# Taps of a state-space convolution: each channel's samples side by side in both factors

## The chip, the cores and the metric

The kernel runs on one core of one Trainium2 chip, as one launch. The metric is the device time of that launch in microseconds, the median of three runs. A core has TensorE (PE in the profile), VectorE (DVE), ScalarE (ACT), GpSimd (POOL) and SyncE (SP). Each works through its own instructions in order, and semaphores tie them together.

## The reference, cut to what matters

Two branches work on the same 2048 x 512 input and are mixed row by row with a sigmoid gate.

```python
g = sigmoid((x * gate_w).sum(-1, keepdims=True))
# branch a: a long convolution, one filter of 2048 taps for each of D = 512 channels
logdA, dB = dt * (A_re + 1j * A_im), dt * (B_re + 1j * B_im)   # (512, 128)
P = exp(logdA[:, :, None] * l)                                 # (512, 128, 2048)
K = einsum("dn,dnl,dn->dl", C, P, dB).real                     # the taps
a = irfft(rfft(u, 2L) * rfft(K, 2L))[:L] + u * Dskip
# branch b: a dense layer of 1792 hidden units
b = gelu(x @ w1 + b1) @ w2 + b2
out = g * a + (1 - g) * b
```

The change concerns the taps `K`. For each channel they are a sum over 128 states of a complex power, and the position l is split in two: l = 64 p + s, with 32 values of p and 64 of s. A power at l is then the product of a power at 64 p (times the coefficients) and a power at s, so that the sum over the states is a matrix product for each channel: 32 rows (p) by 64 columns (s), contracted over 128 states in the partitions, once for the real parts and once for the imaginary parts.

## The kernel before, in words

The program has a front part and a convolution part. In the front part (to about 400 us in the profile) two jobs run beside each other. The dense branch keeps TensorE busy: hidden products (lines 985 to 987, three for each because a factor is split into a high and a low part), a gelu and a cast to the high part on ScalarE (lines 1002 and 1005), the low part on VectorE (line 1012), and output products (lines 1028 to 1031). The other job makes the taps, in 16 groups of 32 channels (`CW`). The convolution part (from about 400 us) transforms taps and signal, multiplies them and transforms back.

One group of taps goes through these functions:

- `phases` (VectorE, line 695): multiples of a state's angle, as integers, in the tile `ph`, 33 samples by 32 channels.
- `waves` (ScalarE, lines 711 to 713): an Abs, a Sin and a second Sin turn the 33 x 32 phases into cosines and sines in the tile `tt`. The last of the three works in place in `tt`.
- `magnitudes` (VectorE, lines 750 and 752; GpSimd, line 740): the magnitudes of the powers, doubled from 2 to 64 samples, in `e`, which is the half `y[:, 1]` of the tile `y`.
- `rotate` (VectorE, lines 763, 770 and 774): magnitude times cosine into `y[:, 0]`, magnitude times sine into `y[:, 1]`.
- `begin` (ScalarE, line 721) and `powers` (VectorE, lines 594 to 597 in `cmul`): the other factor in `xc`, 32 samples by 32 channels for the real and for the imaginary part, doubled from 4 samples to 32. `xc` lies in the rows of `den`; there are two, used in turn. `xt_` and `xv_`, in `loft`, hold the partial products.
- `contract` (TensorE, line 788): for each of the 32 channels two matrix products, with 32 columns of `xc` as the weights and 64 columns of `y` as the moving data. Four channels at a time stand on four tiles of 32 columns of the array. In the profile each product of 32-bit floats is two instructions, so that a group (a block of `contract`) has 32 x 2 x 2 = 128 and there are 2048 in all. They are issued as two tasks of 64, which follow each other in one stretch of 3.84 us.

In the tiles `y`, `xc` and `tt` the sample is the outer index and the channel the inner one: for one channel, two consecutive samples lie 32 words (128 bytes) apart.

The order of the work in the front part is that of a planner: every task has a due time from a table of numbers (`DUES`) and a cost, and a run through the costs settles the order on every engine. A task's instructions are issued in that order, and each waits for its semaphores. The due times, the costs and the tasks' dependencies are the same in the changed kernel.

Of the kernel before, what the change touches and what calls it, by code (L numbers as in the profile page):

```python
# [9 lines left out]
F32 = mybir.dt.float32  # L10
# [7 lines left out]
P = 128  # L18
# [331 lines left out]
def gated_mix(  # L350
# [52 lines left out]
    def front(pool, psum, keep, attic, loft, den, pr):  # L403
# [29 lines left out]
        pus = tiles(N_PU, [P, D], "pu", space=psum)  # L433

        sk = pool.tile([P, 64, 2, 4, 8], F32, name="sk")
        y = pool.tile([P, 2, 64, CW], F32, name="y")
        xc = [den[:, k : k + 4].rearrange("p k d -> p (k d)").rearrange("p (a b c) -> p a b c", a=2, c=CW) for k in (0, 4)]
        xt_, xv_ = (loft[:, k * 1024 : k * 1024 + 1024].rearrange("p (a b c) -> p a b c", a=2, c=CW) for k in range(2))
        tt = loft[:, 2048:4160].rearrange("p (a b c) -> p a b c", a=2, c=CW)
        ph = pool.tile([P, 33, CW], I32, name="phase")  # L440
        zz = pool.tile([P, 2, 5, UW], F32, name="zz")
        x4 = pool.tile([P, 2, 4, UW], F32, name="x4")
# [142 lines left out]
            )  # L585
            vec(UW, lambda: v.tensor_copy(dtb, pus[1][:, 0:UW]), -190, [("pu", 1)], ["dtb"])

        def cmul(due, dst, a, br, bi, n, t, v, ka, kb, kd, kt, kv):

            w = a.shape[-1]  # L590
            br = br.unsqueeze(1).unsqueeze(1).to_broadcast([P, 2, n, w])
            bi = bi.unsqueeze(1).unsqueeze(1).to_broadcast([P, 2, n, w])
            vv, m = nc.vector, n * w
            vec(2 * m, lambda: vv.tensor_mul(t, a, br), due, [ka, *kb], [kt])  # L594
            vec(2 * m, lambda: vv.tensor_mul(v, a, bi), due, [ka, *kb], [kv])  # L595
            vec(m, lambda: vv.tensor_sub(dst[:, 0], t[:, 0], v[:, 1]), due, [kt, kv], [kd])
            vec(m, lambda: vv.tensor_add(dst[:, 1], t[:, 1], v[:, 0]), due, [kt, kv], [kd])
# [110 lines left out]

        def waves(t):
            def sines():  # L710
                nc.scalar.activation(tt[:, 0], ph, AF.Abs)
                nc.scalar.activation(tt[:, 1], ph, AF.Sin, scale=TWO_PI / TURN)
                nc.scalar.activation(tt[:, 0], tt[:, 0], AF.Sin, bias=half_pi, scale=-TWO_PI / TURN)  # L713

            act(3.14, sines, t + D_KA, ["ph"], ["tt"], "sin")

        def begin(c, k, t):

            cs = slice(c * CW, (c + 1) * CW)
            act(  # L720
                0.31, lambda: nc.scalar.copy(xc[k][:, :, 0:4], x4[:, :, :, cs]), t + D_KA,
                ["x4"], [("xc", k)],
            )
# [13 lines left out]
        def magnitudes(u, c, t):  # L737

            cs = slice(c * CW, (c + 1) * CW)
            pl.add("POOL", 0.1, lambda: nc.gpsimd.memset(e[:, 63], 1.0), t, [], ["y1"])  # L740

            def both(lo, step, n):

                a = e[:, lo : lo + n].copy()
                return bass.AP(a.tensor, a.offset, [a.ap[0], [step * CW, 2], *a.ap[1:]])

            def double(k):
                n = 1 << k
                an = ea[u % 2][:, k, cs].unsqueeze(1).unsqueeze(1).to_broadcast([P, 2, n, CW])
                nc.vector.tensor_mul(both(n, 64 - 3 * n, n), both(0, 64 - n, n), an)  # L750

            vec(CW, lambda: nc.vector.tensor_copy(e[:, 0], ea[u % 2][:, 5, cs]), t, [("ea", u % 2)], ["y1"])
            for k in range(5):
                vec(2 * CW << k, lambda k=k: double(k), t, [("ea", u % 2)], ["y1"])

        def rotate(t):

            v = nc.vector
            cc = tt[:, 0, 0:32]
            cc = bass.AP(cc.tensor, cc.offset, [cc.ap[0], [CW, 2], *cc.ap[1:]])  # L760

            def real():
                v.tensor_mul(  # L763
                    y[:, 0].rearrange("p (a b) c -> p a b c", a=2),
                    e.rearrange("p (a b) c -> p a b c", a=2),
                    cc,
                )

            def imag0():
                v.scalar_tensor_tensor(e[:, 0:32], e[:, 0:32], -1.0, tt[:, 1, 0:32], ALU.mult, ALU.mult)  # L770

            vec(64 * CW, real, t, ["tt", "y1"], ["y0"])
            vec(32 * CW, imag0, t, ["tt"], ["y1"])
            vec(32 * CW, lambda: v.tensor_mul(e[:, 32:64], e[:, 32:64], tt[:, 1, 1:33]), t, ["tt"], ["y1"])

        pair = []

        def contract(u, c, k, t):
# [4 lines left out]
            def products(g0):  # L783
                for gg in range(g0, g0 + 4):
                    for r in range(2):
                        for j in range(4):
                            ch = j * 8 + gg
                            nc.tensor.matmul(  # L788
                                pks[q][32 * j : 32 * j + 32, :, gg],
                                x[:, r, :, ch],  # L790
                                y[:, r, :, ch],
                                start=(r == 0),
                                stop=(r == 1),
                                skip_group_check=True,
# [679 lines left out]
```

## Time and profile before

| | |
|---|---|
| median of 3 runs | 508.46 us (508.36 to 508.69) |
| span of the profiled execution | 505.5 us |
| time around that span, against the median | 2.96 us |
| TensorE busy | 495.2 us, 98% of the span |
| VectorE busy | 429.2 us, 85% |
| ScalarE busy | 365.0 us, 72% |
| GpSimd busy | 38.3 us, 8% |
| granted clock of TensorE, mean | 0.996 |

No separate total is kept for the profiled execution, so that its own time is taken as its span and 2.96 us around it, which makes it the median. The profile names an instruction by its line, its engine, and the tile that it writes and those that it reads (out<-in). `den` in such a name can be `xc`, and `loft` can be `tt`, `xt_` or `xv_`, as these share memory. Busy shares over the whole span are means over a front part and a convolution part that have different limits; the stage from 24 to 380 us is the one in which the taps are made. The lengths of TensorE's instructions overlap, and their ends are modelled, so that distances between starts say more than lengths.

### The profile page before, as it was taken

The numbers are of one execution on the slowest core, as the hardware profiler recorded it, in microseconds if no ns is written. First come the engines' busy times: TensorE is split into PE (matmuls) and PEld (weight loads), VectorE is DVE, ScalarE is ACT, GpSimd is POOL, SyncE is SP. The second block draws the span as 40 slices with busy tenths as digits, with TensorE's granted clock in tenths as the row PEclk, the third lists the DMA queues.
The fourth block names the chain that finished last, engine by engine and source line by source line (L and its number), as shares of the span: only waits on it lengthen the run. The fifth ranks groups of instructions, "written<-read, shape, count | busy, mean of one in ns | idle before, by whom it ended". The sixth has DMA issues, their size and how long they took to land.

```text
span 505.5 us, 12181 instructions
## 1 busy us (share of the span) xinstructions
PE 495.2 (98%) x4802; PEld 379.0 (75%) x4802; DVE 429.2 (85%) x817; ACT 365.0 (72%) x632; POOL 38.3 (8%) x78
## 2 busy tenths in 40 slices
PE   8999999999999999999999999999999999999994
PEld 7898888898989889888988888998989522222551
DVE  4977999999999999999999999999940197877455
ACT  6999997899997789997767998636834465565310
POOL 2000000000000000001010020110100100231000
PEclk9999999999999999999999999999999999999998
DMA  8978686531858622855987244950477999989897
GB/s 286 350 280 278 188 243 213 161 126 43 280 138 246 200 73 72 254 168 116 232 217 241 75 64 128 186 100 3 154 219 169 259 389 389 338 305 391 294 344 299
DMA packets 81569, 107.56 MB, mean 213 GB/s; under 512 B 39284, under 2 KB 43784, under 8 KB 80968
## 3 DMA queue, kind: packets, MB, share of 16 engines
q1 hardware_dynamic: 74792, 82.80, 51.8%
q0 software_dynamic: 6016, 20.70, 15.4%
q10 hardware_dynamic: 704, 3.28, 1.8%
q8 instruction: 38, 0.62, 0.5%
q14 instruction: 19, 0.16, 0.1%
HBM read 61.14 MB, written 45.62 MB: 211 GB/s over the span
## 4 chain that ended last, share of the span: by engine, by line
PE 93%; DMA 2%; SPq 1%; DVE 1%; issue 1%; ACT 0%; POOL 0%; DVEq 0%; POOLq 0%
PE pk L788 12%; PE ph L985 10%; PE acc L1028 10%; PE ph L987 10%; PE ph L986 10%; PE acc L1029 9%; PE acc L1031 9%; PE p2k L1218 5%; PE p2u L1218 5%; PE pa L1257 3%; PE ph L489 3%; PE pb L1373 2%; DMA tk<-tk_d 1%; SPq L830 1%; DMA tk_d<-sk 1%; PE acc L1101 1%
## 5 line engine op out<-in xcount | busy, mean ns | idle before, releaser
L985 PE MATMUL ph<-xh,wh 128*128 128x256 f32 x448 | 127.5, 285 | 0.0
L987 PE MATMUL ph<-xh,wl 128*128 128x256 f32 x448 | 126.8, 283 | 0.0
L986 PE MATMUL ph<-xlo,wh 128*128 128x256 f32 x448 | 126.7, 283 | 0.0
L985 PEld LDWEIGHTS ph<-xh,wh 128*128 128x128 f32 x448 | 85.2, 190 | 6.9 <-issue 4.0
L986 PEld LDWEIGHTS ph<-xlo,wh 128*128 128x128 f32 x448 | 85.1, 190 | 2.1
L987 PEld LDWEIGHTS ph<-xh,wl 128*128 128x128 f32 x448 | 85.2, 190 | 0.0
L1028 PE MATMUL acc<-wh,hh 128*128 128x512 f32 x208 | 84.3, 405 | 0.0
L1029 PE MATMUL acc<-wl,hh 128*128 128x512 f32 x208 | 81.7, 393 | 0.0
L1031 PE MATMUL acc<-wh,hl 128*128 128x512 f32 x208 | 81.4, 391 | 0.0
L1002 ACT ACTIVATE ph<-ph,b1t 128x256 f32<-128x256 f32 x112 | 50.5, 451 | 25.0 <-PE ph L987 23.2
L788 PE MATMUL pk<-y,den 128*32 128x64 f32 x2048 | 61.4, 290 | 0.0
L788 PEld LDWEIGHTS pk<-y,den 128*32 128x32 f32 x2048 | 57.2, 136 | 2.6 <-issue 0.7
L1012 DVE TENSOR_TENSOR hl<-ph,hh 128x512 fp32r<-128x512 f32 (+1 forms) x62 | 38.2, 618 | 18.3 <-ACT hh L1005 10.8
L1028 PEld LDWEIGHTS acc<-wh,hh 128*128 128x128 f32 x208 | 39.1, 188 | 19.4 <-issue 8.8
L750 DVE TENSOR_TENSOR y<-y,ea 128x64 f32<-128x64 f32 (+4 forms) x80 | 45.3, 566 | 0.8 <-POOL y L740 0.3
L1031 PEld LDWEIGHTS acc<-wh,hl 128*128 128x128 f32 x208 | 39.1, 188 | 8.8
L1029 PEld LDWEIGHTS acc<-wl,hh 128*128 128x128 f32 x208 | 39.1, 188 | 6.1
L1226 ACT COPY k<-p2k 128x512 f32<-128x512 f32 x32 | 18.6, 586 | 27.2 <-issue 11.3
L594 DVE TENSOR_TENSOR loft<-den,zz 128x256 f32<-128x256 f32 (+2 forms) x48 | 37.2, 774 | 0.2
L595 DVE TENSOR_TENSOR loft<-den,zz 128x256 f32<-128x256 f32 (+2 forms) x48 | 37.2, 775 | 0.1
L763 DVE TENSOR_TENSOR y<-y,loft 128x2048 f32<-128x2048 f32 x16 | 36.6, 2286 | 0.4 <-ACT loft L713 0.2
L1005 ACT CAST hh<-ph 128x512 fp32r<-128x512 f32 (+1 forms) x62 | 33.0, 533 | 4.3 <-PE acc L1029 2.4
(197 smaller groups left out, 873.3 us busy)
## 6 DMA issues: line engine op xcount, KB each, us to landing
tk_d<-sk SPq DMA_DIRECT2D x32, 256.0 KB, 5.3
t_d<-sa SPq DMA_DIRECT2D x32, 256.0 KB, 5.1
tu_d<-attic SPq DMA_DIRECT2D x40, 128.0 KB, 3.5
attic<-in_xt_dram SPq DMA_DIRECT2D x16, 256.0 KB, 4.3
attic<-in_xs_dram SPq DMA_DIRECT2D x16, 256.0 KB, 5.0
xl_d<-xlo SPq DMA_DIRECT2D x8, 512.0 KB, 5.9
xh_d<-xh SPq DMA_DIRECT2D x8, 512.0 KB, 3.9
out_dram<-io SPq DMA_DIRECT2D x16, 256.0 KB, 3.1
```

Source lines behind the costliest of these rows:

```text
L594: vec(2 * m, lambda: vv.tensor_mul(t, a, br), due, [ka, *kb], [kt])
L750: nc.vector.tensor_mul(both(n, 64 - 3 * n, n), both(0, 64 - n, n), an)
L788: nc.tensor.matmul(pks[q][32 * j : 32 * j + 32, :, gg], x[:, r, :, ch], y[:, r, :, ch], start=(r == 0), stop=(r == 1), skip_group_check=True,)
L985: nc.tensor.matmul(p, h, xh[xk][:, d], start=(d == 0), stop=False)
L986: nc.tensor.matmul(p, h, xlo[xk][:, d], start=False, stop=False)
L987: nc.tensor.matmul(p, lo, xh[xk][:, d], start=False, stop=(d == 3))
L1002: nc.scalar.activation(phs[q][:, n], phs[q][:, n], AF.Gelu_apprx_tanh, bias=b1t[:, f : f + 1])
L1012: nc.vector.tensor_sub(lo, phs[q][:, 0:nf], hi.bitcast(F32))
L1028: nc.tensor.matmul(a, h, wh[1][w], start=start, stop=False, skip_group_check=seeded)
L1029: nc.tensor.matmul(a, h, wl[1][w], start=False, stop=False, skip_group_check=seeded)
L1031: nc.tensor.matmul(a, l, wh[1][w], start=False, stop=stop, skip_group_check=seeded)
L1218: nc.tensor.matmul(out[64 * i : 64 * i + 64], w, x, start=True, stop=True)
```

## The change

Channel and sample change places in `y`, `xc`, `xt_`, `xv_` and `tt`: the channel is now the outer index, and the samples of one channel lie side by side. The phases stay as they were, sample by channel; the first two instructions of `waves` read them as before and write their results turned, so that consecutive elements of their output lie 33 words (132 bytes) apart. `begin` turns the four starting samples in the same manner, 32 words apart. In `cmul` and `magnitudes` the factor that is the same for all samples of a channel is now repeated in the innermost index and no longer over whole rows of channels. The doubling steps of `magnitudes` and `powers` write runs of 1, 2, 4, 8 and 16 samples per channel, where they wrote runs of 32 channels. `contract` reads 32 weights and 64 moving columns side by side.

No instruction is added or taken away, and on every engine all instructions stand in the same order as before.

```diff
-        y = pool.tile([P, 2, 64, CW], F32, name="y")
-        xc = [den[:, k : k + 4]....rearrange("p (a b c) -> p a b c", a=2, c=CW) for k in (0, 4)]
-        xt_, xv_ = (loft[...].rearrange("p (a b c) -> p a b c", a=2, c=CW) for k in range(2))
-        tt = loft[:, 2048:4160].rearrange("p (a b c) -> p a b c", a=2, c=CW)
+        y = pool.tile([P, 2, CW, 64], F32, name="y")
+        xc = [den[:, k : k + 4]....rearrange("p (a c b) -> p a c b", a=2, c=CW) for k in (0, 4)]
+        xt_, xv_ = (loft[...].rearrange("p (a c b) -> p a c b", a=2, c=CW) for k in range(2))
+        tt = loft[:, 2048:4160].rearrange("p (a c b) -> p a c b", a=2, c=CW)
...
-        def cmul(due, dst, a, br, bi, n, t, v, ka, kb, kd, kt, kv):
-            w = a.shape[-1]
-            br = br.unsqueeze(1).unsqueeze(1).to_broadcast([P, 2, n, w])
-            bi = bi.unsqueeze(1).unsqueeze(1).to_broadcast([P, 2, n, w])
+        def cmul(due, dst, a, br, bi, n, t, v, ka, kb, kd, kt, kv, inner=False):
+            w = CW if inner else a.shape[-1]
+            shape, at = ([P, 2, w, n], 3) if inner else ([P, 2, n, w], 1)
+            br = br.unsqueeze(1).unsqueeze(at).to_broadcast(shape)
+            bi = bi.unsqueeze(1).unsqueeze(at).to_broadcast(shape)
...
         def waves(t):
             def sines():
-                nc.scalar.activation(tt[:, 0], ph, AF.Abs)
-                nc.scalar.activation(tt[:, 1], ph, AF.Sin, scale=TWO_PI / TURN)
+                to = [tt[:, i].rearrange("p c b -> p b c") for i in range(2)]
+                nc.scalar.activation(to[0], ph, AF.Abs)
+                nc.scalar.activation(to[1], ph, AF.Sin, scale=TWO_PI / TURN)
                 nc.scalar.activation(tt[:, 0], tt[:, 0], AF.Sin, bias=half_pi, scale=-TWO_PI / TURN)
...
-                0.31, lambda: nc.scalar.copy(xc[k][:, :, 0:4], x4[:, :, :, cs]), t + D_KA,
+                0.31, lambda: nc.scalar.copy(xc[k][:, :, :, 0:4].rearrange("p a c b -> p a b c"), x4[:, :, :, cs]), t + D_KA,
...
                 cmul(
-                    t, x[:, :, n : 2 * n], x[:, :, 0:n], zz[:, 0, i, cs], zz[:, 1, i, cs], n,
-                    xt_[:, :, 0:n], xv_[:, :, 0:n], ("xc", k), ["zz"], ("xc", k), "xt", "xv",
+                    t, x[:, :, :, n : 2 * n], x[:, :, :, 0:n], zz[:, 0, i, cs], zz[:, 1, i, cs], n,
+                    xt_[:, :, :, 0:n], xv_[:, :, :, 0:n], ("xc", k), ["zz"], ("xc", k), "xt", "xv", True,
                 )
...
-                return bass.AP(a.tensor, a.offset, [a.ap[0], [step * CW, 2], *a.ap[1:]])
+                return bass.AP(a.tensor, a.offset, [a.ap[0], [step, 2], *a.ap[1:]])
...
-                an = ea[u % 2][:, k, cs].unsqueeze(1).unsqueeze(1).to_broadcast([P, 2, n, CW])
+                an = ea[u % 2][:, k, cs].unsqueeze(1).unsqueeze(3).to_broadcast([P, 2, CW, n])
...
-            vec(CW, lambda: nc.vector.tensor_copy(e[:, 0], ea[u % 2][:, 5, cs]), t, [("ea", u % 2)], ["y1"])
+            vec(CW, lambda: nc.vector.tensor_copy(e[:, :, 0], ea[u % 2][:, 5, cs]), t, [("ea", u % 2)], ["y1"])
...
-                                x[:, r, :, ch],
-                                y[:, r, :, ch],
+                                x[:, r, ch],
+                                y[:, r, ch],
```

`rotate` has the same three instructions on the turned tiles: the cosine of sample b is read for the samples b and 32 + b at once, the second with an offset of one sample.

More of the change, by code (lines that the diff above doesn't have):

```diff
@@ L435, in front @@
         sk = pool.tile([P, 64, 2, 4, 8], F32, name="sk")
-        y = pool.tile([P, 2, 64, CW], F32, name="y")
-        xc = [den[:, k : k + 4].rearrange("p k d -> p (k d)").rearrange("p (a b c) -> p a b c", a=2, c=CW) for k in (0, 4)]
-        xt_, xv_ = (loft[:, k * 1024 : k * 1024 + 1024].rearrange("p (a b c) -> p a b c", a=2, c=CW) for k in range(2))
-        tt = loft[:, 2048:4160].rearrange("p (a b c) -> p a b c", a=2, c=CW)
+        y = pool.tile([P, 2, CW, 64], F32, name="y")
+        xc = [den[:, k : k + 4].rearrange("p k d -> p (k d)").rearrange("p (a c b) -> p a c b", a=2, c=CW) for k in (0, 4)]
+        xt_, xv_ = (loft[:, k * 1024 : k * 1024 + 1024].rearrange("p (a c b) -> p a c b", a=2, c=CW) for k in range(2))
+        tt = loft[:, 2048:4160].rearrange("p (a c b) -> p a c b", a=2, c=CW)
         ph = pool.tile([P, 33, CW], I32, name="phase")
```

16 lines of the change are left out of this document (8 added, 8 removed).

## The prediction

> **What bounds the kernel now.** I read the page's totals first, then the busy time by stage, then groups of instructions by shape, then single places on the time line, then the waits.
>
> ```profile
> span 505.5 us, 12181 instructions
> PE 495.2 (98%) x4802; PEld 379.0 (75%) x4802; DVE 429.2 (85%) x817; ACT 365.0 (72%) x632; POOL 38.3 (8%) x78
> ...
> 24.00:60.00 36.00, 35.97 (x244) 32.15 (x242) 30.67 (x76) 35.35 (x62) 0.53 (x1) 1.00 0.80 265
> 60.00:100.00 40.00, 40.00 (x488) 32.74 (x472) 39.61 (x84) 34.15 (x55) 0.25 (x2) 1.00 0.67 205
> 100.00:140.00 40.00, 40.00 (x500) 35.53 (x492) 39.17 (x81) 38.98 (x71) 0.30 (x2) 1.00 0.47 149
> 140.00:180.00 40.00, 40.00 (x471) 34.64 (x471) 39.51 (x74) 30.34 (x50) 1.85 (x5) 1.00 0.66 181
> 180.00:220.00 40.00, 40.00 (x481) 34.87 (x480) 39.16 (x70) 39.29 (x75) 1.30 (x4) 1.00 0.50 153
> 220.00:260.00 40.00, 40.00 (x379) 33.43 (x378) 39.15 (x80) 29.94 (x48) 5.86 (x9) 1.00 0.74 178
> 260.00:300.00 40.00, 40.00 (x588) 36.11 (x587) 38.04 (x69) 34.95 (x62) 2.59 (x7) 1.00 0.47 134
> 300.00:340.00 40.00, 40.00 (x360) 35.24 (x360) 39.31 (x80) 27.23 (x43) 6.50 (x10) 1.00 0.65 135
> 340.00:380.00 40.00, 40.00 (x591) 34.92 (x590) 31.38 (x51) 24.02 (x36) 3.12 (x6) 1.00 0.45 130
> ```
>
> The columns are the window, then TensorE, its weight loads, VectorE, ScalarE and GpSimd busy, the granted clock and the DMA. The share over the span (VectorE 85%, ScalarE 72%) hides what matters: from 24 to 380 us, the stage that the change touches, TensorE is never idle, and from 60 to 340 us VectorE is busy for 273.95 of 280 us (39.61 + 39.17 + 39.51 + 39.16 + 39.15 + 38.04 + 39.31). So two engines are full at once, and the third, ScalarE, is full in two windows (38.98 and 39.29 of 40). Its 61.75 us of idle time from 24 to 380 lie in the others. The chain of waits runs over TensorE for 93%, but time saved on TensorE alone is worth no more than VectorE's idle time, 6.05 us in those seven windows.
>
> **The change part by part.** No instruction is added, removed or put elsewhere; only access patterns differ. So every term is a count of elements by a price per element. The rows by shape:
>
> ```profile
> L788 PE MATMUL pk<-y,den 128*32 128x64 f32 x2048 | 61.4, 290 | 0.0
> L763 DVE TENSOR_TENSOR y<-y,loft 128x2048 f32<-128x2048 f32 x16 | 36.6, 2286 | 0.4 <-ACT loft L713 0.2
> L594 DVE TENSOR_TENSOR loft<-den,zz 128x1024 f32<-128x1024 f32 x16 | 19.5, 1221 | 0.1
> L774 DVE TENSOR_TENSOR y<-y,loft 128x1024 f32<-128x1024 f32 x16 | 19.5, 1219 | 0.0
> L713 ACT ACTIVATE loft<-loft,half_pi 128x1056 f32<-128x1056 f32 x16 | 18.7, 1169 | 0.0
> L712 ACT ACTIVATE loft<-phase 128x1056 f32<-128x1056 int32 x16 | 17.5, 1094 | 0.2
> L711 ACT ACTIVATE loft<-phase 128x1056 f32<-128x1056 int32 x16 | 17.5, 1093 | 0.0
> L1269 ACT COPY sa<-pa 128x512 f32<-128x512 f32 x32 | 17.2, 589 | 9.5 <-PE pa L1257 5.4 <-issue 4.1
> L815 ACT COPY sk<-ph 128x512 f32<-128x512 f32 x8 | 4.7, 593 | 0.0
> L659 ACT ACTIVATE loft<-loft 128x768 f32<-128x768 f32 x4 | 3.4, 854 | 0.0
> L721 ACT COPY den<-x 128x256 f32<-128x256 f32 x16 | 6.2, 407 | 11.5 <-PE pk L788 8.1 <-DVE x L597 3.4
> ```
>
> And six pieces of TensorE's time line (start, length, line):
>
> ```profile
> 71.61 3.84 PE L788 MATMUL pk<-y,den 128*32 128x64 f32 x128
> 99.08 0.65 PE L489 MATMUL ph<-s,c1t 32*64 32x512 f32 x2
> 99.10 0.65 PE L489 MATMUL pk<-s,c1t 32*64 32x512 f32 x2
> 99.11 0.66 PE L489 MATMUL pu<-s,c1t 32*64 32x512 f32 x4
> 420.85 1.03 PE L1218 MATMUL p2k<-t,cc 128*64 128x512 f32 x4
> 421.71 1.03 PE L1218 MATMUL p2k<-t,f 128*64 128x512 f32 x4
> ```
>
> *TensorE.* A block of L788 is 128 instructions on four column tiles, 32 each, 64 columns each: 2048 columns per tile. Less the last one's 0.29 us the block takes 3.55 us, so 1.73 ns per column, and each column is read 128 bytes from the one before. L1218 reads columns side by side: four instructions on two tiles start 0.86 us apart from the next four, so 1024 columns per tile in 0.86 us, 0.84 ns each. At that price a block is 2048 x 0.84 = 1.72 us, and 1.83 us shorter: 29.3 us of TensorE's time over 16 blocks. The other end is nothing, if the pace is that of issue: 3.55 / 128 = 28 ns per instruction. I take the gain, since L489 issues eight instructions between 99.08 and 99.11 us, far faster than 28 ns each.
>
> [...]
>
> *What a hop costs.* From the same rows: an element that lies far from the one before costs 1.73 ns on a read, where neighbours cost 0.84 on TensorE, 1.04 on VectorE ((2286 - 1219) / 1024) and 0.83 on ScalarE ((1094 - 854) / 288). No row shows a write that hops at every element; L815 writes runs of eight at 593 ns against 589 for L1269 in one run, so runs cost nothing.
>
> *ScalarE.* L711 and L712 now write 1056 elements each with 132 bytes from one to the next, L721 256 elements with 128 bytes. L713 stays in one run. If a hopping write is bound like the hopping read, the extra is 1.73 - 0.83 = 0.90 ns: 2 x 1056 x 0.90 + 256 x 0.90 = 2.13 us in each of 16 groups, 34.1 us in all. The other end is nothing. I take 0.90: 1.73 ns is twice what TensorE needs for neighbours, so I read it as a limit of the memory that is read and not of the engine, and such a limit should hold for a write too.
>
> [...]
>
> *What of it reaches the end.* ScalarE is off the chain only as long as it keeps ahead. Its groups of sines by window, and what stands behind one:
>
> ```profile
> 24.00:60.00 36.00, 1.09 (x1) 1.00 0.80 265
> 100.00:140.00 40.00, 2.19 (x2) 1.00 0.47 149
> 180.00:220.00 40.00, 1.11 (x1) 1.00 0.50 153
> 260.00:300.00 40.00, 2.34 (x3) 1.00 0.47 134
> ...
> 152.10 1.16 ACT L713 ACTIVATE loft<-loft,half_pi 128x1056 f32<-128x1056 f32 x1
> 154.58 0.93 ACT L1002 ACTIVATE ph<-ph,b1t 128x256 f32<-128x256 f32 x2
> 155.54 0.59 ACT L1005 CAST hh<-ph 128x512 fp32r<-128x512 f32 x1
> ...
> DVE hl L1012 <- ACT hh L1005: 10.8, 9, 3.5
> ACT ph L1002 <- PE ph L987: 23.2, 12, 6.0
> ACT io L1053 <- PE acc L1031: 10.8, 10, 4.0
> ```
>
> Lower end: each window first uses up its own idle time. 24-60: 2.13 against 0.65 idle; 100-140: 4.26 against 1.02; 180-220: 2.13 against 0.71; 260-300: 6.39 against 5.05. The overflows are 1.48 + 3.24 + 1.42 + 1.34 = 7.5 us; the other windows hold it. Upper end: all 34.1. Behind each group of sines stand the gelu (L1002) and the cast (L1005) of the dense part; VectorE's L1012 and TensorE's L1028 and L1031 wait for them. VectorE works in order and has no idle time to make up a lost microsecond, and it already waits for that cast (10.8 us in nine waits). Much of ScalarE's idle time is its wait for TensorE (23.2 and 10.8 us), which moves along when TensorE is late. So I take two thirds, 23 us.
>
> *VectorE.* L752 (32 elements) now writes single elements and the smallest L750 (64) reads and writes them: (32 + 128) x (1.73 - 1.04) ns = 0.11 us, 1.8 us over 16 groups, from 0 to twice that. The other L750 and L594/L595 keep runs of 2 to 16 in their long operands, which I cost at nothing by L815, but their factor is now read n times over before the next one. No row shows a word read again and again in the innermost place; a factor repeated over whole rows costs nothing (L594 1221 against L774 1219). Bounds: 0, and 0.69 ns for each of 128 + 256 + 512 + 1024 + 2 x (256 + 512 + 1024) = 5504 elements, 3.8 us per group, 61 us. I take 0, as the nearest row is L594. The rotations (L763, L770, L774) read rows of 33 words in runs of 32: nothing.
>
> *Sum.* 505.5 + 23 (ScalarE) + 1.8 (VectorE) = 530.3; off it goes what the shorter blocks give, at most VectorE's 6.05 us less its own 1.8, of which I count 3: 527.3 us of span. The runs' median is 508.46, 2.96 above this execution's span, so 530 us. Blocks shorter by 29 us of TensorE are hidden behind VectorE; what is late next is the hidden layer's cast.
>
> **The rivals.**
>
> *ScalarE's writes hop for free* (the other side). Then only TensorE's blocks change and VectorE decides. The point from which it decides is the price of a hopping write: under about 0.1 ns extra, 4 us over 16 groups, all hidden. The time is 508.5 - 6.05 + 1.8 = 504, and 502 if VectorE's small steps cost nothing. For it: no row shows a write of that kind to be slow. Against it: the reads' 1.73 ns. [...]
>
> *The repeated factor costs VectorE.* 61 us of VectorE work less 6 of idle: 508.5 + 55 = 563, and ScalarE then has time to hide its own. For it: single elements cost on the other reads; against it: the same word lies in the same place.
>
> *The change does not do what it says*: blocks of L788 stay at 3.8 us because issue sets them. With free writes 508.5 + 1.8 = 510, with ScalarE's price 533.
>
> **How the numbers follow.** ScalarE's price as taken: 0.52, of itself from 514 (7.5 us passed on, less 3) to 545 (34.1 and 1.8), likeliest 530. Free writes and shorter blocks: 0.24, 502 to 507. Free writes and unchanged blocks: 0.06, about 508 to 510. The repeated factor: 0.14, 555 to 575. The rest, 0.04, is a hop price well above 1.73 ns. The range of 503 to 545 leaves out the repeated factor and the rest. 0.2%, about 1 us, is what a measurement of this kernel can tell from no change. Faster: 0.24 and a little of the unchanged blocks, 0.26. Same: 0.05. Slower: 0.69.
>
> **What would show it.** L711 and L712 near 2.0 us (1094 + 1056 x 0.90), L721 near 0.64, L713 still 1.17. L788's blocks near 2.0 us with 128 instructions. L750 with 64 elements near 0.3 us, its larger shapes and L594/L595 unchanged. TensorE with idle time before L1028 and L1031, put down to ScalarE or VectorE, and VectorE's wait for L1005 above 10.8 us. Wrong if L711 stays near 1.1 us (then 504), or if L594 with 1024 elements goes towards 1.9 us (then 563).

## The result, and the profile after

| | before | after |
|---|---|---|
| median of 4 runs | 508.57 us (508.36 to 509.12) | 527.04 us (524.96 to 528.95) |
| span of the profiled execution | 505.5 us | 523.2 us |

The kernel is slower: the ratio is 1.0369 (95% interval 1.0334 to 1.0404), 18.5 us. The profiled execution of after took 524.96 us by its own clock, 1.76 us around its span. In the changed kernel the lines from 594 to 710 are one further on than before (L594 is now L595), and the lines from 711 on two (L711 is L713, L788 is L790, L1005 is L1007). In the experiments lines are up to three further on than before in the same manner.

The totals of the page and the chain that ended last, then TensorE, weight loads, VectorE, ScalarE and GpSimd busy with granted clock from 60 to 340 us:

```profile
span 523.2 us, 12185 instructions
PE 479.7 (92%) x4802; PEld 352.2 (67%) x4802; DVE 430.7 (82%) x817; ACT 400.5 (77%) x632; POOL 38.7 (7%) x78
ACT 46%; PE 29%; DVE 11%; issue 6%; DMA 4%; SPq 1%; POOL 0%; ACTq 0%; DVEq 0%; POOLq 0%
60.00:340.00 280.00, 251.99 (x3031) 207.21 (x3032) 259.36 (x498) 257.03 (x390) 15.10 (x32) 0.99 0.55 156
```

The chain ran over TensorE for 93% before; now ScalarE has 46% of it and TensorE 29%. The counts of these engines' instructions are as before; the four more in the total (12185 against 12181) are none of theirs. ScalarE works 35.5 us more in all (400.5 against 365.0), VectorE 1.5 us more, TensorE 15.5 us less. From 60 to 340 us TensorE was busy for all 280 us and VectorE for 273.95; now they are busy for 252 and 259. Both have idle time, and ScalarE isn't full over the whole stretch either (257.03 of 280). So no single engine is the limit by its total: all three wait for one another, and ScalarE's lateness is handed round. The groups by shape show where its time comes from (busy time, mean ns of one, then the idle time ahead):

```profile
L713 ACT ACTIVATE loft<-phase 128x1056 f32<-128x1056 int32 x16 | 36.0, 2249 | 1.3 <-DVE phase L696 1.3
L714 ACT ACTIVATE loft<-phase 128x1056 f32<-128x1056 int32 x16 | 35.8, 2236 | 0.2
L715 ACT ACTIVATE loft<-loft,half_pi 128x1056 f32<-128x1056 f32 x16 | 18.2, 1140 | 0.0
L723 ACT COPY den<-x 128x256 f32<-128x256 f32 x16 | 10.2, 675 | 3.8 <-DVE x L598 3.4 <-PE pk L790 0.4
L790 PE MATMUL pk<-y,den 128*32 128x64 f32 x2048 | 32.8, 220 | 4.1 <-DVE y L776 2.2 <-ACT attic L507 1.7
L595 DVE TENSOR_TENSOR loft<-den,zz 128x1024 f32<-128x1024 f32 x16 | 19.5, 1219 | 0.1
L752 DVE TENSOR_TENSOR y<-y,ea 128x1024 f32<-128x1024 f32 x16 | 19.5, 1218 | 0.1
L752 DVE TENSOR_TENSOR y<-y,ea 128x64 f32<-128x64 f32 x16 | 4.3, 269 | 0.3
L754 DVE COPY y<-ea 128x32 f32<-128x32 f32 x16 | 3.1, 194 | 0.0
```

The two writes that hop 132 bytes at each element went from 1093 and 1094 to 2249 and 2236 ns; L715, which writes the same tile in one run, stayed (1169 before, 1140 now). The extra is (2249 - 1093) / 1056 = 1.09 ns an element, and in `begin` (675 - 407) / 256 = 1.05. Lengths say a little too much here, since ScalarE's instructions overlap (the two rows of before below by 0.11 us, those of after by 0.26). A group whose sines follow each other directly, of before and of after on the time line:

```profile
127.70 1.10 ACT L711 ACTIVATE loft<-phase 128x1056 f32<-128x1056 int32 x1
128.69 1.09 ACT L712 ACTIVATE loft<-phase 128x1056 f32<-128x1056 int32 x1
```

```profile
134.17 2.27 ACT L713 ACTIVATE loft<-phase 128x1056 f32<-128x1056 int32 x1
136.18 2.28 ACT L714 ACTIVATE loft<-phase 128x1056 f32<-128x1056 int32 x1
```

From start to start it is 0.99 us and 2.01 us: (2.01 - 0.99) / 1056 = 0.97 ns an element is what the next instruction feels. This is so for the second of the two in every group, but for the first in this group alone: in the other 15 an ACT_TABLE_LOAD of 1.28 us stands between the two and starts only when the first has ended, so that the first costs its whole length there. ScalarE's busy time, in which an overlap counts once, grew by 35.5 us where the lengths of the three groups grew by 40.8. VectorE's products with the factor repeated in the innermost place (L595, and L752 with 1024 elements) kept their 1219 ns. TensorE's blocks took 3.84 us before; on the time line (start, length) the first and the last of them are now

```profile
76.30 2.01 PE L790 MATMUL pk<-y,den 128*32 128x64 f32 x128 [1.74 <-ACT attic L507]
390.99 1.99 PE L790 MATMUL pk<-y,den 128*32 128x64 f32 x128
```

so TensorE did gain (61.4 - 32.8) = 28.6 us of work, and yet the last block starts at 390.99 where it started at 372.74. The waits (who, for whom, us in total, times, longest) say who held whom:

```profile
DVE hl L1014 <- ACT hh L1007: 15.3, 14, 3.5
DVE phase L704 <- ACT loft L714: 7.2, 8, 1.5
PE acc L1033 <- DVE hl L1014: 4.1, 5, 1.2
PE ph L987 <- DVE hl L1014: 4.1, 5, 1.5
PE ph L987 <- ACT sk L817: 4.1, 3, 1.7
DVE y L765 <- ACT loft L715: 3.8, 3, 2.3
PE acc L1030 <- ACT hh L1007: 3.3, 3, 1.3
```

VectorE's wait for the cast of the hidden layer grew from 10.8 to 15.3 us; two waits for the sines themselves came with it (7.2 and 3.8 us). L704 begins the phases of the next group and overwrites what L713 and L714 read; L765 uses what L715 writes. TensorE, never idle here before, stands behind VectorE's `hl` and behind ScalarE.

### The profile page after: what moved, and what is told of

Same layout as the page of the kernel before. It is cut to its first block, busy times and chain, and to the rows that moved or that the text cites. A ratio compares the mean times of both kernels' runs of the same rounds, so it can differ in the third digit from the quotient of the medians.

```text
span 523.2 us, 12185 instructions
## 1 busy us (share of the span) xinstructions
PE 479.7 (92%) x4802; PEld 352.2 (67%) x4802; DVE 430.7 (82%) x817; ACT 400.5 (77%) x632; POOL 38.7 (7%) x78
## 4 chain that ended last, share of the span: by engine, by line
ACT 46%; PE 29%; DVE 11%; issue 6%; DMA 4%; SPq 1%; POOL 0%; ACTq 0%; DVEq 0%; POOLq 0%
ACT loft L713 6%; ACT loft L714 5%; ACT ph L1004 5%; PE p2k L1220 5%; PE p2u L1220 5%; ACT L1004 4%; PE pa L1259 3%; ACT hh L1007 3%; ACT L714 3%; ACT loft L715 2%; PE ph L987 2%; ACT io L1055 2%; PE ph L989 2%; PE ph L988 2%; DVE y L765 2%
## 5 line engine op out<-in xcount | busy, mean ns | idle before, releaser
L1030 PE MATMUL acc<-wh,hh 128*128 128x512 f32 x208 | 85.3, 410 | 8.0 <-ACT hh L1007 3.3
L1033 PE MATMUL acc<-wh,hl 128*128 128x512 f32 x208 | 82.9, 398 | 4.2 <-DVE hl L1014 4.1
L1030 PEld LDWEIGHTS acc<-wh,hh 128*128 128x128 f32 x208 | 39.5, 190 | 27.6 <-issue 9.3
L1014 DVE TENSOR_TENSOR hl<-ph,hh 128x512 fp32r<-128x512 f32 (+1 forms) x62 | 38.2, 617 | 23.5 <-ACT hh L1007 15.3
L1033 PEld LDWEIGHTS acc<-wh,hl 128*128 128x128 f32 x208 | 39.3, 189 | 17.3 <-DVE hl L1014 9.0
L752 DVE TENSOR_TENSOR y<-y,ea 128x64 f32<-128x64 f32 (+4 forms) x80 | 46.1, 576 | 0.6
L765 DVE TENSOR_TENSOR y<-y,loft 128x2048 f32<-128x2048 f32 x16 | 36.6, 2287 | 4.0 <-ACT loft L715 3.8
L596 DVE TENSOR_TENSOR loft<-den,zz 128x256 f32<-128x256 f32 (+2 forms) x48 | 37.1, 773 | 1.1 <-ACT den L723 0.9
L595 DVE TENSOR_TENSOR loft<-den,zz 128x256 f32<-128x256 f32 (+2 forms) x48 | 37.1, 774 | 0.3
L713 ACT ACTIVATE loft<-phase 128x1056 f32<-128x1056 int32 x16 | 36.0, 2249 | 1.3 <-DVE phase L696 1.3
L790 PE MATMUL pk<-y,den 128*32 128x64 f32 x2048 | 32.8, 220 | 4.1 <-DVE y L776 2.2
L714 ACT ACTIVATE loft<-phase 128x1056 f32<-128x1056 int32 x16 | 35.8, 2236 | 0.2
```

Source lines behind the costliest of these rows:

```text
L713: nc.scalar.activation(to[0], ph, AF.Abs)
L714: nc.scalar.activation(to[1], ph, AF.Sin, scale=TWO_PI / TURN)
L765: v.tensor_mul(y[:, 0].rearrange("p c (a b) -> p a c b", a=2), e.rearrange("p c (a b) -> p a c b", a=2), cc,)
L1030: nc.tensor.matmul(a, h, wh[1][w], start=start, stop=False, skip_group_check=seeded)
L1033: nc.tensor.matmul(a, l, wh[1][w], start=False, stop=stop, skip_group_check=seeded)
```

## The experiments

They ask three things: is the loss the price of ScalarE's hop and how much of it is passed on, what is TensorE's gain worth, and can the gain be had without the price. Ratios are to runs of the kernel before that were taken beside each set: their median is 509.02 us for e1, e2, e4 and e8, 508.26 for e3, e5, e6 and e9, 507.52 for e10 to e12, and 506.94 for e13. As it differs by up to 2 us from set to set, a difference between runs of two sets is good to about a microsecond.

### Is it the hop? The same kernel with straight writes (e1)

```diff
-                to = [tt[:, i].rearrange("p c b -> p b c") for i in range(2)]
+                to = [tt[:, i].rearrange("p c b -> p (c b)").rearrange("p (b c) -> p b c", c=CW) for i in range(2)]
```

> The changed kernel, but ScalarE's first two sine instructions write their results in the order in which they read the phases, so that no element hops (the values in the sines' tile then belong to other samples, which leaves the turning out). begin still writes its 256 elements 128 bytes apart. Theory A (the loss is the price of ScalarE's hopping writes): the two instructions fall from 2.24 to 1.09 us, and the time falls below that of before, to 503 to 507 us, since TensorE's blocks stay at 2.05 us but VectorE is full. Rival B (the new layout costs elsewhere, in VectorE's short runs, in TensorE's reads or in the waits): the time stays above 515 us.

Measured: 500.67 us (499.25 to 502.07), ratio 0.9839 (0.9806 to 0.9872): faster than before by 8.4 us (a little more than expected), and 26.4 us faster than after (27.0 by the ratios). The groups of sines, and the row from 60 to 340 us:

```profile
L713 ACT ACTIVATE loft<-phase 128x1056 f32<-128x1056 int32 x16 | 17.4, 1090 | 2.0 <-DVE phase L696 2.0
L714 ACT ACTIVATE loft<-phase 128x1056 f32<-128x1056 int32 x16 | 17.4, 1087 | 0.2
60.00:340.00 280.00, 267.02 (x3369) 223.88 (x3370) 277.92 (x534) 241.28 (x406) 19.17 (x39) 1.00 0.59 163
```

ScalarE's busy time falls from 400.5 to 367.5 us: 33.0 us of its work went, and 26.4 us of the time, so that about 80% of it had been passed on. What limits now is VectorE, busy for 277.92 of 280 us. So the loss is the hop's, and everything else of the change together is a gain.

### The hop alone in the kernel before (e2)

```diff
-                nc.scalar.activation(tt[:, 0], ph, AF.Abs)
-                nc.scalar.activation(tt[:, 1], ph, AF.Sin, scale=TWO_PI / TURN)
+                to = [tt[:, i].rearrange("p b c -> p (b c)").rearrange("p (c b) -> p b c", c=CW) for i in range(2)]
+                nc.scalar.activation(to[0], ph, AF.Abs)
+                nc.scalar.activation(to[1], ph, AF.Sin, scale=TWO_PI / TURN)
```

> The kernel before, with the one difference that the first two sine instructions write to the turned addresses (132 bytes from one element to the next); everything else keeps its layout, so that the values are those of other samples. Theory A: each of the two takes 2.24 us, 36.6 us more of ScalarE's work in 16 groups; nearly all of it is passed on, since here TensorE's blocks stay at 3.84 us and neither TensorE nor VectorE can make anything up: 530 to 545 us. Rival C (ScalarE's idle time, 62 us from 24 to 380 us, takes up what its full windows do not): 515 to 520 us. Rival B: within 2 us of 508.5.

Measured: 530.13 us (527.78 to 531.61), ratio 1.0414 (1.0375 to 1.0452), 21.1 us over before. One of the two groups, and VectorE's wait for the cast, which was 10.8 us:

```profile
L712 ACT ACTIVATE loft<-phase 128x1056 f32<-128x1056 int32 x16 | 37.1, 2320 | 1.1 <-DVE phase L695 1.1
DVE hl L1013 <- ACT hh L1006: 16.3, 14, 3.5
```

About the same price and the same wait as in after, with TensorE's blocks long as before. ScalarE is busy for 399.5 us, 34.5 more than before, of which 61% were passed on: the time lies at the lower end of theory A, and not "nearly all" of the work came through. From here to after (1.0369) TensorE's shorter blocks and the rest are worth 2.3 us (0.0045 of 509), and the two intervals overlap, so that it may be nothing; beside straight writes they are worth 8 to 10. As long as ScalarE is late, TensorE's time is hardly wanted.

### TensorE's reads alone (e4), then with VectorE relieved (e5, e6)

```diff
-                                x[:, r, :, ch],
-                                y[:, r, :, ch],
+                                x[:, r].rearrange("p b c -> p (b c)")[:, 32 * ch : 32 * ch + 32],
+                                y[:, r].rearrange("p b c -> p (b c)")[:, 64 * ch : 64 * ch + 64],
```

> The kernel before, with the one difference that the products of the taps read 32 weights and 64 moving columns in one run (the elements of other channels and samples, the layout in memory is as before). Theory A: the 16 blocks fall from 3.84 to 2.05 us, 28.6 us of TensorE's work, but VectorE is busy for 98% of the stage, so that the time falls by 2 to 6 us only, to 502 to 507 us. Rival D (TensorE alone bounds the stage): 480 us. Rival E (the blocks stay at 3.8 us unless something else of the change is there too): 508.5 us.

Measured: 498.70 us (498.39 to 498.80), ratio 0.9799 (0.9775 to 0.9824), 10.3 us faster, for 28.6 us of TensorE's work, and more than the 2 to 6 us expected. Is VectorE what keeps the other 18? e5 is the kernel before with half of L763's products left out, e6 has that and e4's edit:

```diff
-                v.tensor_mul(
-                    y[:, 0].rearrange("p (a b) c -> p a b c", a=2),
-                    e.rearrange("p (a b) c -> p a b c", a=2),
-                    cc,
-                )
+                v.tensor_mul(y[:, 0, 0:32], e[:, 0:32], tt[:, 0, 0:32])
```

> The kernel before with less VectorE work: the first instruction of each rotation makes 1024 of its 2048 products (the other half keeps what stood there), 1.07 us less in each of 16 groups, 17 us of VectorE's time. Theory A (TensorE and VectorE are both full, and with the long blocks TensorE decides): 507 to 509 us, no change. Rival H (VectorE alone decides): 491 to 495 us.

> The kernel before with both: the products of the taps read in runs (28.6 us less of TensorE's work, which alone gave 498.7 us) and the rotation's first instruction makes half of its products (17 us less of VectorE's work). Theory A (the rest of TensorE's gain was hidden behind VectorE): 483 to 491 us, so that 17 us off VectorE are worth 8 to 15 us here and nothing without the shorter blocks. Rival I (the rest of the gain is hidden behind ScalarE or the transfers): 496 to 499 us.

Measured: e5 507.74 us (506.87 to 509.40), ratio 0.9998 (0.9982 to 1.0015), no change; e6 492.03 us (490.52 to 493.43), ratio 0.9683 (0.9641 to 0.9725). The rows from 60 to 340 us of e4, e5 and e6:

```profile
60.00:340.00 280.00, 267.68 (x3387) 224.66 (x3387) 278.06 (x535) 239.31 (x408) 18.73 (x39) 1.00 0.59 164
60.00:340.00 280.00, 280.00 (x3236) 242.42 (x3221) 261.38 (x530) 234.75 (x400) 18.73 (x38) 1.00 0.58 162
60.00:340.00 280.00, 272.23 (x3430) 228.89 (x3430) 271.86 (x553) 242.84 (x414) 18.80 (x39) 1.00 0.59 164
```

In e4 VectorE is full (278.06) and TensorE not (267.68); in e5 TensorE is full (280.00) and VectorE not. So VectorE's 17.1 us (36.6 - 19.5) are worth nothing while TensorE is full, and about 6 us once it is not (6.7 by the medians, 5.9 by the ratios). They were expected to be worth 8 to 15: in e6 no engine is full (272, 272 and 243 of 280), and what is left is waits between them, as in after.

### Half of the hop (e3)

The kernel after, in which only the Abs writes turned and the first Sin writes straight.

```diff
-                nc.scalar.activation(to[1], ph, AF.Sin, scale=TWO_PI / TURN)
+                nc.scalar.activation(tt[:, 1].rearrange("p c b -> p (c b)").rearrange("p (b c) -> p b c", c=CW), ph, AF.Sin, scale=TWO_PI / TURN)
```

> The changed kernel with one hop in place of two: the Abs writes turned, the first Sin writes in the order in which it reads (the sines are those of other samples). ScalarE has 1.16 us per group, 18.5 us in all, more than in the run with both written straight (500.7 us). Theory A1 (what is passed on grows faster than the work, since small delays fit into the leads that ScalarE has over VectorE and TensorE): 504 to 510 us, well under half of the 26.4 us between the two. Rival A2 (the same share of each microsecond is passed on, 26.4 of 36.9): 512 to 516 us.

Measured: 511.21 us (508.77 to 512.12, 10 runs), ratio 1.0054 (1.0035 to 1.0073). That is 10.5 us above e1, where both hops cost 26.4. ScalarE is busy for 385.2 us; the first 17.7 us of its work (385.2 - 367.5) cost 10.5, the other 15.3 (400.5 - 385.2) cost 15.8. Each theory's figure missed by a little: a part is hidden, and the more ScalarE is loaded, the less. The two instructions are now of unequal length:

```profile
L713 ACT ACTIVATE loft<-phase 128x1056 f32<-128x1056 int32 x16 | 35.9, 2247 | 1.6 <-DVE phase L696 1.6
L714 ACT ACTIVATE loft<-phase 128x1056 f32<-128x1056 int32 x16 | 17.4, 1090 | 0.2
```

### The hop elsewhere: on ScalarE's read (e8), on GpSimd (e9)

Both make the whole of the changed kernel's computation. e8 reads the phases turned and writes straight:

```diff
-                nc.scalar.activation(to[0], ph, AF.Abs)
-                nc.scalar.activation(to[1], ph, AF.Sin, scale=TWO_PI / TURN)
+                turned = ph.rearrange("p b c -> p c b")
+                nc.scalar.activation(tt[:, 0], turned, AF.Abs)
+                nc.scalar.activation(tt[:, 1], turned, AF.Sin, scale=TWO_PI / TURN)
```

> The changed kernel, but ScalarE reads the phases in the turned order (128 bytes from one element to the next) and writes the sines in one run. The computation is whole. Theory A with one price for any hop at the memory: about 2.1 to 2.25 us for each of the two instructions and 522 to 529 us. Rival F (only a hopping write costs ScalarE): 1.09 us each and 503 to 507 us. Rival G (a hopping read costs ScalarE what it cost TensorE, 1.73 ns per element): 2.04 us each and 518 to 524 us.

In e9 GpSimd copies the phases turned first, and ScalarE reads and writes in runs:

```diff
+                turned = tt[:, 1].bitcast(I32)
+                nc.gpsimd.tensor_copy(turned, ph.rearrange("p b c -> p c b"))
+                nc.scalar.activation(tt[:, 0], turned, AF.Abs)
+                nc.scalar.activation(tt[:, 1], turned, AF.Sin, scale=TWO_PI / TURN)
```

> The changed kernel, but GpSimd turns the phases: it copies them into the sines' tile, channel by channel, and ScalarE reads and writes them in one run. The computation is whole. The copy waits for the rotation before (its tile is in use until then), and the sines wait for the copy. GpSimd is busy for 8% only. Theory A (any place is good for the turning that isn't ScalarE or VectorE): 499 to 504 us, as in the run with both written straight, if the copy takes up to 3 us. Rival J (the copy takes longer, or stands in GpSimd's queue behind its transfers' waits, and the sines come late): 508 to 530 us. The spans of GpSimd say which of the two.

Measured: e8 526.95 us (526.02 to 527.44), ratio 1.0352 (1.0319 to 1.0385), as after; e9 540.25 us (539.35 to 541.60), ratio 1.0638 (1.0601 to 1.0675), above both of its figures. The first group of sines in e8; then, of e9, the copy, the sines, ScalarE's wait, the page's totals, and a copy on the time line with VectorE's instruction beside it:

```profile
L713 ACT ACTIVATE loft<-phase 128x1056 f32<-128x1056 int32 x16 | 35.1, 2192 | 1.3 <-DVE phase L696 1.3
```

```profile
L713 POOL COPY loft<-phase 128x1056 int32<-128x1056 int32 x16 | 43.3, 2709 | 130.6 <-DVE y L777 60.9 <-DVE phase L696 48.7 <-ACT st L507 21.0
L714 ACT ACTIVATE loft<-loft 128x1056 f32<-128x1056 int32 x16 | 17.4, 1087 | 37.1 <-POOL loft L713 37.1
ACT loft L714 <- POOL loft L713: 37.1, 14, 4.9
PE 490.8 (91%) x4802; PEld 359.0 (67%) x4802; DVE 457.7 (85%) x817; ACT 368.9 (69%) x632; POOL 80.6 (15%) x94
63.26 2.69 POOL L713 COPY loft<-phase 128x1056 int32<-128x1056 int32 x1 [10.84 <-DVE phase L696]
63.85 2.65 DVE L596 TENSOR_TENSOR loft<-den,zz 128x512 f32<-128x512 f32 x1
```

A hopping read costs ScalarE (2192 - 1093) / 1056 = 1.04 ns extra an element, nearly what the write costs. GpSimd has the time for the copy (2709 ns, 43.3 us in all), but it costs in two places. ScalarE works in order and stands before it for 37.1 us: its own work fell back to 368.9 us, and the copy's length lies in the path of each group. And VectorE, which has no time to spare, is held up: its same 817 instructions are busy for 457.7 us, against 430.7 in after. The L596 of 512 elements above takes 2.65 us, where such instructions take 0.68, and ends 0.55 us after the copy. Between 20 and 420 us, 13 of VectorE's instructions take 1 us or more longer than others of their form; each runs beside a copy and ends 0.1 to 1.1 us after it. So in this trace GpSimd's copy holds VectorE up. How much of the loss is ScalarE's wait and how much VectorE's, no run separates.

### Which of TensorE's operands matters (e10, e12)

e10 is the kernel before with `xc` turned and all that belongs to it (as in the change), `y`, `tt`, the sines and the rotations as before; in e12 it is only the moving columns that are read as a run:

```diff
-                                x[:, r, :, ch],
+                                x[:, r, ch],
```

> The whole computation, with only the factor xc turned (with xt_, xv_, begin and powers as in the kernel after); y, tt, the sines, magnitudes and rotate stay as before. ScalarE then hops on 256 elements a group only: 16 x 0.27 = 4.3 us of its work. Theory M (the 64 moving columns set the pace of a block, and the weights are loaded beside them): L788's blocks stay at 3.8 us, and the time is 508 to 511 us. Theory W (the 32 hopping weights set it, or as much of it as the columns): the blocks fall to 2.0 us (W alone) or to about 3.2 us (both in turn, by 96 reads an instruction), and since VectorE is full behind them the time is 498 to 503 us, faster than before.

```diff
-                                y[:, r, :, ch],
+                                y[:, r].rearrange("p b c -> p (b c)")[:, 64 * ch : 64 * ch + 64],
```

> The kernel before, with L788's 64 moving columns read as one run (wrong values), and its 32 weights read 128 bytes apart as before. Theory M: the blocks fall from 3.84 to about 2.0 us, as when both are runs, time about 498.7. Theory W: they stay near 3.8. Both in turn: about 2.6.

Measured: e10 507.08 us (505.80 to 508.51), ratio 1.0001 (0.9984 to 1.0019), no change; e12, a single run, 499.99 us against 507.52. A block of each:

```profile
72.15 3.75 PE L789 MATMUL pk<-y,den 128*32 128x64 f32 x128
```

```profile
72.35 2.14 PE L788 MATMUL pk<-y,den 128*32 128x64 f32 x128
```

The weights in runs make 0.09 us of a block, the moving columns 1.70. The change's turning of `xc` was not needed for its gain.

### How near is near enough (e11)

The kernel after with two other patterns: the first two sines write to every second word, and the moving columns are read as 32 pairs of neighbours, the pairs 256 bytes apart.

```diff
-                to = [tt[:, i].rearrange("p c b -> p b c") for i in range(2)]
+                to = [loft[:, 2048:4160].rearrange("p (n i) -> p i n", i=2)[:, i] for i in range(2)]
...
-                                y[:, r, ch],
+                                y[:, r].rearrange("p c b -> p (c b)").rearrange("p (m c j) -> p c m j", m=32, j=2)[:, ch],
```

> The kernel after, with two patterns changed for a look at the lengths alone (wrong values): the first two sines read as after and write to every second word (8 bytes apart, over 2112 words), and L790's moving columns are read as 32 pairs of neighbours, the pairs 256 bytes apart. If ScalarE's price belongs to any write that is not next to the one before: L713 and L714 stay near 2240 ns. If it belongs to far hops (132 bytes): near 1090 ns, and the time falls towards 500 to 505. For the columns: if a hop costs 0.9 ns once a pair, the block is about 2.0 + 0.92 = 2.9 us; if pairs are as good as a run, 2.0; if every read that isn't in a long run pays, 3.8.

Measured (one run, 505.42 us; its Abs also waits for the last rotation, 4.3 us, since it writes over both halves of `tt`):

```profile
L713 ACT ACTIVATE loft<-phase 128x1056 f32<-128x1056 int32 x16 | 19.9, 1245 | 5.8 <-DVE y L776 4.3 <-DVE phase L696 1.4
L714 ACT ACTIVATE loft<-phase 128x1056 f32<-128x1056 int32 x16 | 18.9, 1182 | 0.2
72.74 2.02 PE L790 MATMUL pk<-y,den 128*32 128x64 f32 x128
```

Writes 8 bytes apart cost ScalarE 0.14 and 0.09 ns extra an element ((1245 - 1093) / 1056 and (1182 - 1094) / 1056), where 132 bytes cost 1.09. And pairs of words are as good for TensorE's moving columns as a run of 64: 2.02 us against 2.01.

On ScalarE, then, 8 bytes' distance is nearly free, and 128 (the read of e8, 1.04 ns) or 132 bytes are not. No step between 8 and 128 bytes was run, so that these runs do not show where the price sets in.

### A version from this: pairs (e13)

The moving data needn't be turned, only paired. The real half of `y` holds the samples b and 32 + b of a channel side by side; VectorE's first rotation writes it so, and nothing of ScalarE's changes.

```diff
+        yp = y[:, 0].rearrange("p s c -> p (s c)").rearrange("p (b c h) -> p h b c", h=2, c=CW)
...
-                    y[:, 0].rearrange("p (a b) c -> p a b c", a=2),
+                    yp,
...
+                            o = pks[q][32 * j : 32 * j + 32, :, gg]
...
-                                pks[q][32 * j : 32 * j + 32, :, gg],
+                                o if r else o.rearrange("p (h b) -> p b h", h=2),
                                 x[:, r, :, ch],
-                                y[:, r, :, ch],
+                                y[:, r, :, ch] if r else yp[:, :, :, ch].rearrange("p h b -> p b h"),
```

> The whole computation. The kernel before, with one edit: y[:, 0], the real half of the moving data, lies as [sample b][channel][half h] for the sample 32 h + b, so that L788 (here some lines on) reads it as 32 pairs of neighbours 256 bytes apart; VectorE's first rotation (L763) writes to every second word (8 bytes apart); ScalarE, the weights and y[:, 1] stay as before. If pairs are read at the price of a run, half of a block's instructions get short, and a block falls from 3.8 us to about 2.95 us, 14 us of TensorE's time in all. Theory P (VectorE's write 8 bytes apart costs at most what ScalarE's did, 0.15 ns an element): L763 stays within 2290 to 2600 ns, up to 5 us of VectorE's work in all, and the time is 499 to 505 us, faster than before. Theory Q (any write of VectorE's that isn't beside the last one costs 0.7 ns, as in the smallest magnitudes of the kernel after): L763 goes to 3700 ns, 23 us more of VectorE's work, which has 6 us idle: 520 to 526 us.

Measured: 499.68 us (499.38 to 500.83, 5 runs), ratio 0.9855 (0.9829 to 0.9880): 7.3 us faster than before, and faster than after. The rotation, a block, the last block, and the row from 60 to 340 us:

```profile
L764 DVE TENSOR_TENSOR y<-y,loft 128x2048 f32<-128x2048 f32 x16 | 36.6, 2286 | 0.4 <-ACT loft L713 0.2
72.57 3.18 PE L790 MATMUL pk<-y,den 128*32 128x64 f32 x128
366.83 3.14 PE L790 MATMUL pk<-y,den 128*32 128x64 f32 x128
60.00:340.00 280.00, 278.10 (x3360) 238.15 (x3362) 278.02 (x536) 239.30 (x407) 18.60 (x38) 1.00 0.59 164
```

VectorE's write 8 bytes apart costs nothing (2286 ns before, 2286 now). Half of a block's instructions in pairs shorten it by 0.66 us rather than 0.9; why not the whole half stays open. The weights still hop (half of e12's 1.70 us would be 0.85), and the same edit makes these instructions write their results by turns to two places; no run has that alone. The 10.9 us of TensorE's work that this saves (61.4 - 50.5) bring 7.3 us, where e4's 28.6 bring 10.3: VectorE is full now (278.02 of 280). The imaginary half in pairs was not run: it would have VectorE work in place at every second word, and e4 suggests some 3 us at most for it.

## Why the prediction was right, point by point

530 us were predicted with a range of 503 to 545, and slower at 0.69; 527.04 came.

**What bounds.** Right: two engines were full at once, and ScalarE nearly full in two windows. e5 shows the one half of it (VectorE relieved by 17 us: no change), e4 the other (TensorE relieved by 28.6: 10.3 us).

**TensorE's blocks.** 2.0 us were expected, 2.01 came. The rival in which issue sets the pace falls: 128 instructions in 2.01 us are 16 ns each, under the 28 ns of before. That is across four column tiles; on one tile an instruction has four times that (63 ns), so that no run shows whether issue would set a pace within a tile.

**The price of a hop.** 0.90 ns extra an element were taken, from TensorE's hopping read; 1.09 came on the sines and 1.05 in `begin`. 2.0 us were expected of L711 and L712 (2.25 and 2.24 came) and 0.64 of L721 (0.675). As the overlap takes some of it back (0.97 from start to start where the next instruction follows at once), 34.1 us were expected in all and 35.5 came. The reasoning, a limit of the memory and not of the engine, was the author's reading of the rows, and no run shows the limit itself. It has support in that TensorE's reads of moving columns (1.73 ns in place of 0.84), ScalarE's reads (1.04 ns extra, e8) and ScalarE's writes (1.09 ns extra) all pay at a word per hop, and that pairs free the first (2.02 us a block, e11) and 8 bytes nearly free the last (0.09 to 0.14 ns extra, e11). TensorE's hopping weights are the exception: they cost only 0.09 us of a block (e10).

The rival with free writes falls with it: where an element of a run takes ScalarE 0.83 ns ((1094 - 854) / 288), a write that hops 132 bytes makes 1.92 ns of it (0.83 + 1.09).

**What is passed on.** 23 us, two thirds, were taken; e1 against after gives 26.4 of 33.0 (80%), and in the kernel before e2 gives 21.1 of 34.5 (61%). Some of the 26.4 may come by way of TensorE's clock, which is 0.986 in three of after's four runs and 0.996 to 0.999 in e1's (see the last section); no run separates it. The lower end of 7.5 us rests on a misread row: from 260 to 300 us the view counts three groups, but the third begins at the window's very end (the kernel before, start and length),

```profile
299.84 1.09 ACT L711 ACTIVATE loft<-phase 128x1056 f32<-128x1056 int32 x1
```

so that two groups (4.26 us) fit into the 5.05 us of idle time and the lower end is about 6.1. The places were right: VectorE's wait for the cast grew, and TensorE stands before L1030 and L1033. Not named was VectorE's wait before it overwrites the phases that a sine still reads (`phase L704`, 7.2 us).

**TensorE's gain.** This is the term that was mis-sized as the prediction states its limit: 3 us, at most VectorE's 6.05. Beside the hop it is 2.3 us or less with VectorE's steps in it, so that the sum came out, but with straight writes it is 10.3 (e4). That the sum came within about 3 us of the time is partly luck: by e1 the change without the sines' hop gains 8.4 us, where the sum has 1.2 (3 less 1.8), and the hop then costs 26.4 where the sum has 23. The two misses go opposite ways. The bound was VectorE's idle time from 60 to 340 us alone. In e4 the last block starts at 366.3 instead of 372.7, 6.4 us earlier, about as that bound has it; but the block itself, 1.8 us shorter, stands where VectorE is no longer full, and the span ends 8.7 us earlier (496.8 against 505.5). The 10.3 us of the medians are more than that, as the profiled execution of before was a quick one: the seven runs of before beside e4 have spans of 505.0 to 508.2 us, with a median of 506.4, and e4's four have 496.6 to 496.9.

**VectorE.** 1.8 us were taken for its steps of single elements; the 64-element step grew by 269 - 220 = 49 ns and the copy by 194 - 174 = 20, 1.1 us in 16 groups. The factor repeated in the innermost place was taken as free and is, 1219 ns; the rival of 563 us falls.

**Around the span.** 2.96 us were added; all four runs of after show 1.7 to 1.8, and the seven runs of before beside e1 show 1.8 to 2.9. The term set the median of several runs against the span of one. So the spans agree less well than the times: 527.3 expected, 523.2 profiled, 524.9 to 527.2 in the other runs.

## What to carry to other kernels

An engine's layout gain can be paid by whoever writes the layout (here ScalarE, 1.09 ns an element): price the hop on the writer before the run on the reader, and ask whether the writer has the idle time in the stage concerned. If the work goes to a third engine, look at every engine's lengths afterwards: in e9 it was VectorE's that grew (busy for 457.7 us against 430.7). A full transposition may be more than the reader needs; here two neighbouring words gave it the whole rate (2.02 us a block against 2.01, e11), and an index order that pairs far samples let the engine that writes anyway do so for nothing (2286 ns before and in e13). When two engines are full at once, ask what idle time the other one has. Here TensorE had none in the full stage, and relieving VectorE alone was worth nothing (507.74 us against 508.26, e5); VectorE had 6.05 us, and relieving TensorE alone brought a little more than that (10.3 us, e4).

## What the runs showed of the hardware

ScalarE pays for a hop of 132 bytes at every element on the write (1.09 ns) as on a read of 128 bytes (1.04 ns), and hardly at 8 bytes (0.09 to 0.14); VectorE's write at 8 bytes is free (2286 ns in both). A copy on GpSimd holds VectorE's instructions up (e9: 2.65 us instead of 0.68). And one pause of TensorE had a slower stretch behind it: in after it waits for VectorE from 127.9 us, starts again at 129.91, and from 130.5 runs at half the clock for 3.4 us.

```profile
129.91 0.64 PE L489 MATMUL ph<-attic,c1t 32*64 32x512 f32 x1 [2.00 <-DVE hl L1014]
130.50:133.90 3.40, 3.40 (x22) 2.08 (x7) 3.26 (x9) 3.39 (x7) 0.00 (x0) 0.50 0.40 116
131.93 0.63 PE L1031 MATMUL acc<-wl,hh 128*128 128x512 f32 x1
134.23 0.39 PE L1031 MATMUL acc<-wl,hh 128*128 128x512 f32 x1
214.05 0.64 PE L489 MATMUL ph<-attic,c1t 32*64 32x512 f32 x1 [2.28 <-DVE hl L1014]
214.00:217.40 3.40, 2.71 (x22) 1.28 (x22) 2.77 (x6) 3.37 (x12) 0.00 (x0) 1.00 0.46 123
```

The first line has the 2.00 us of idle time ahead, the second the granted clock (0.50) of the stretch, the next two the same product within it and after it, 0.63 and 0.39 us long. The last two show a longer pause, 2.28 us, with the full clock (1.00) behind it; two more, of 2.20 us up to 60.65 and 2.15 us up to 260.72, were not followed by the half clock either. So the length alone does not decide. In e9 a pause of only 1.49 us, up to 101.24, has long products behind it at once: L489 takes 1.11 us there, where it took 0.65 at 99.08 us in before. What decides stays open. The other three runs of after show a mean clock of 0.986 against this one's 0.993 and take 1.6 to 4.0 us longer; that more such stretches make the difference is likely, but they have no trace. In e9, with pauses of up to 3.4 us, the mean clock is 0.968.
